# Attention and channel mix on one core: the first batch worked in halves of its heads

## The chip, the cores and the metric

The kernel runs on one core of a Trainium2 chip. The metric is the device time of one execution in microseconds; the median of the runs is compared. The engines are PE (TensorE), ACT (ScalarE), DVE (VectorE), POOL (GpSimd) and SP (SyncE, which only issues DMAs here). PE writes into PSUM, which the kernel divides into two rings of tiles: three `s` tiles of 2 x 512 columns and two `mm` tiles of 512.

## The reference

Two layers follow each other. The first is attention with a mask by blocks of 64, over 8 batches of 8 heads, 576 tokens and 64 dimensions; the second mixes each token with the one before it and runs through two matrices with a squared relu and a sigmoid gate:

```python
scores = scale * np.matmul(q, k.transpose(0, 1, 3, 2))
scores = np.where(block_i >= block_j, scores, -1000000000.0)
attn = np.exp(scores - np.max(scores, axis=-1, keepdims=True))
attn = attn / (np.sum(attn, axis=-1, keepdims=True) + 1e-09)
x = np.matmul(attn, v)                      # heads side by side: 512 channels
...
xk = mu_k * x + (1.0 - mu_k) * x_prev
xr = mu_r * x + (1.0 - mu_r) * x_prev
k = np.maximum(xk @ w_k, 0.0)
v = k * k @ w_v
r = 1.0 / (1.0 + np.exp(-(xr @ w_r)))
out = r * v
```

## The kernel before, in words

The work is cut into some 950 named tasks, each on one engine. For each batch there are, in order of dependence:

- loads of q and k (SP, two of each, 576 KB, each with four heads) and of v; they go to a ring of six `ld` tiles, and a load waits until the cast that read its tile before is done;
- casts to 16 bit (L255 and L251, on POOL, DVE or ACT, into `nl` and `vo` tiles);
- "turns" (L367): nine PE transposes of a q or k tile into an `s` tile, and a copy out of it into `qkt` (one of 1152 columns, for batch 0 two of 576);
- scores (L431): 12 tasks of four or eight 64x64 matmuls, each into an `s` tile, and the exponential of each on ACT (L441), which frees the tile;
- sums (`av S`, L483): 60 matmuls with a matrix `pick` of ones, that leave the row sums of the exponentials in part of one `s` tile; then products with v (`av A`, `av B`, L492), 40 matmuls each, in two further `s` tiles;
- on DVE: the sums turned (L520), reciprocals (L525), copies between partitions (L255/L251), per product a transpose that spreads them (L551) and the norm that multiplies (L561 and L565) into `xt`;
- the token differences (L587, DVE or POOL) and the mixes into XK and XR (L603, DVE): one instruction for each of four groups of 128 channels.

For batch 0 the 12 score tasks are two times six: the first six need only the first half of each copied turn. All 12 stand ahead of the one set of sums.

The second layer works on chunks of 512 tokens. A chunk has eight key products (`pk`, L650: four matmuls with WK into an `mm` tile, then relu and square), four gate products (`pr`, L672, then a tanh on ACT) and four value products (`pv`, L700: eight matmuls with WV, then the output on DVE, L708, and a store). The first key product needs the mixes of all four channel groups of batch 0 and two of the four casts of w_k.

What sets the order is a table, `ORDER`: task numbers in the order in which they are issued. Each engine takes its own tasks in that order and waits at each for what it needs; so a waiting instruction holds all that stands behind it on its engine. `PLACE` is a string that names the engine of each task that may go to several. A number with "+n" in `ORDER` puts n dummy matmuls on an identity (L264) ahead of that task on PE. Tasks of the kinds in `SHARED` (differences, mixes, squares, casts, copies of reciprocals) are tied: one on POOL waits for the last such one on DVE that was issued ahead of it.

Of the kernel before, what the change touches and what calls it, by code (L numbers as in the profile page):

```python
# [24 lines left out]
3 4 5+9 13 14 7 15+1 18 19 0 6 20+5 22 8 9 21 17 104 10+2 12 63+2 1 11  # L25
64 61 62 67+1 68 105 16 47+1 48 57+1 58 106 107 69 70 59 60 49+1 50 55
56 53 54 29 100 101 96 97 98+1 99 25 30 26 51 52 65+1 66 102 92 93 94 2
95 71 74 75 77 23 24 103 112 113 73 80 122 123 76 114+2 115 81 165 166
72+4 78 79 157 158 87 90 126 127 120+7 121 167 116 168 134 117 27 28
124+2 31 82 88 125 83 85 118+1 119 91 32 33 34 557 558 135 554 555 132  # L30
133 86 161 162 128 129 130 84 569 570 159 160 563 169 170 564 571 566
163 171 572 37 131 136 567 559 35 164 36 172 108 109 179 568 180 197 198
573 89 551 552 139 38 560 140 141 143 191 142 574 192 561 137 144 45 46
577 578 556 110 581 199 200 582 111 41 42 553 138 145 146 565 562 181
182 575 576 579 580 177 195 196 43 44 185 186 178 39 40 238 589 152 147
150 148 590 155 189 187 188 583 584 149 183 193 242 190 243 586 587 153
239 151 184 295 230 194 244 245 592 593 231 173 234 174 201 204 240 156
598 599 205 154 613 614 241 307 206 235 232 233 610 611 612 616 600 299
236 617 618 619 207 620 615 607 608 595 609 175 591 588 237 208 202 596
597 308 258 209 176 259 601 602 621 622 604 605 603 260 261 296 303 304  # L40
606 300 203 210 211 221 369 226 212 266 585 623 624 267 625 626 309 248
633 634 310 227 256 252 253 213 217 219 223 630 631 257 262 263 250 264
265 663 664 251 228 297 298 636 246 594 272 273 222 637 249 268 254 225
255 627 363 628 657 658 220 360 629 313 214 224 364 301 215 632 269 270
438 635 361 362 271 305 306 642 659 643 644 274 276 302 331 639 332 640
660 661 329 330 645 646 654 655 277 278 279 216 218 317 638 280 283 284
665 666 318 247 662 314 656 648 649 366 290 651 652 653 365 650 281 229
641 647 333 334 275 282 667 677 668 678 674 675 311 370 337 439 338 335
336 315 316 371 669 670 285 286 432 289 367 368 287 671 672 291 327 328
319 293 321 322 707 708 288 680 681 320 292 325 294 326 323 683 684 685  # L50
312 695 696 686 687 688 324 689 690 698 699 700 339 342 390 391 382 383
704 705 691 692 693 694 706 343 344 679 345 433 340 380 381 346 347 701
711 712 341 429 430 702 703 440 435 676 394 395 709 350 710 697 490 713
714 348 349 355 384 378 379 388 724 725 389 726 715 392 385 398 393 372
716 717 436 437 358 396 399 721 397 353 376 356 351 386 377 718 722 387
739 740 719 400 742 743 354 736 737 733 727 734 359 357 735 728 352 755
738 744 756 403 404 405 407 373 741 431 434 467 374 673 465 466 468 751
752 729 745 746 406 493 449 450 747 375 401 408 411 445 446 682 730 494
748 443 749 750 496 402 451 731 732 452 409 410 753 762 754 455 456 763
764 457 458 463 464 420 422 426 499 795 796 428 421 491 444 412 765 425  # L60
766 414 453 454 757 758 416 413 759 459 460 419 424 447 448 461 760 761
441 462 768 780 781 427 769 500 469 472 497 782 423 473 417 474 418 792
793 777 778 774 775 789 790 791 779 475 495 720 797 798 415 471 478 479
# [718 lines left out]
```

## Time and profile before

| | |
|---|---|
| median of 3 runs | 258.75 us (258.35 to 261.7) |
| the profiled execution | 258.47 us, of which 256.7 us are the profile's span |
| PE busy | 245.5 us (96%), 2710 matmuls, 41 of them dummies |
| DVE busy | 191.9 us (75%) |
| ACT busy | 178.8 us (70%) |
| POOL busy | 95.0 us (37%) |
| DMA | 46.96 MB, mean 183 GB/s |

PE's busy share is high in every slice, also in the first ones, where dummies and waits for data lie between its matmuls; it is 78 to 91% in the four stretches of 10 us up to 40 us, and over 95% after them but for the last. The granted TensorE clock is full throughout. To read the time, one asks from when PE's work is unbroken, what stands ahead of that moment, and where PE waits later.

### The profile page before, as it was taken

Reading aid. Unit: us, or ns where it says so; the run is one execution under the profiler, and the core shown is the slowest. Engines: PE = TensorE matmul, PEld = TensorE weight load, DVE = VectorE, ACT = ScalarE, POOL = GpSimd, SP = SyncE. Lnnn points to the kernel's source line nnn. Section 1 sums busy time; section 2 is a strip of 40 time slices with the busy share of each in tenths; the row PEclk is TensorE's granted clock in tenths of the full one; section 3 lists DMA queues with packets and bytes.
Section 4 is the critical chain, followed back from the end, with each engine's and each line's share of the span. In section 5 each row is a group of like instructions: output and inputs, shape, how many; then the busy total and the mean of one; then the engine's idle time right before and its main releaser. Section 6 shows DMA issues by size and latency. Waiting matters only on the chain.

```text
span 256.7 us, 6535 instructions
## 1 busy us (share of the span) xinstructions
PE 245.5 (96%) x2710; PEld 121.7 (47%) x2710; DVE 191.9 (75%) x275; ACT 178.8 (70%) x247; POOL 95.0 (37%) x81
## 2 busy tenths in 40 slices
PE   7887989999999999999999999999999989999995
PEld 3445535544655455444554545454444544444443
DVE  2535999999899989979696899757985786654313
ACT  1597786999868868859788678796789820550630
POOL 1122636773076015540533048306411362420730
PEclk9999999999999999999999999999999999999999
DMA  7999977999899919997951999759917004003104
GB/s 246 363 253 251 368 275 186 280 343 263 266 300 207 223 44 252 228 221 152 252 108 41 234 203 242 169 127 237 183 68 190 4 0 166 0 1 123 43 23 182
DMA packets 93150, 46.96 MB, mean 183 GB/s; under 512 B 80696, under 2 KB 80960, under 8 KB 93120
## 3 DMA queue, kind: packets, MB, share of 16 engines
q1 hardware_dynamic: 93120, 46.54, 74.6%
q8 instruction: 21, 0.34, 0.6%
q14 instruction: 9, 0.07, 0.1%
HBM read 33.56 MB, written 9.44 MB: 168 GB/s over the span
## 4 chain that ended last, share of the span: by engine, by line
PE 79%; DVE 10%; DMA 6%; issue 2%; ACT 1%; SPq 0%; DVEq 0%
PE t_mm L650 24%; PE t_mm L700 23%; PE t_mm L672 12%; PE t_s L431 7%; PE t_s L492 7%; DMA t_ld<-in_q_dram 4%; PE t_s L483 4%; PE t_s L367 3%; DMA t_ld<-in_k_dram 3%; DVE t_rt L551 2%; DVE XK L603 2%; DVE t_qkt L255 1%; DVE t_xt L565 1%; DVE t_d L587 1%; DVE WV L256 1%
## 5 line engine op out<-in xcount | busy, mean ns | idle before, releaser
L441 ACT ACTIVATE t_e<-t_s 128x1024 f16<-128x1024 f32 (+1 forms) x96 | 88.3, 983 | 19.2 <-PE t_s L431 17.1
L650 PE MATMUL t_mm<-XK,WK 128*128 128x512 f16 x288 | 68.5, 379 | 0.4 <-DVE XK L603 0.3
L638 POOL TENSOR_TENSOR t_k<-t_kr 128x512 f16<-128x512 f32 x39 | 42.1, 1097 | 69.5 <-ACT t_kr L628 51.4
L700 PE MATMUL t_mm<-WV,t_k 128*128 128x512 f16 (+1 forms) x296 | 66.5, 374 | 0.1
L628 ACT ACTIVATE t_kr<-t_mm 128x512 f32<-128x512 f32 x57 | 33.8, 598 | 24.8 <-PE t_mm L650 24.0
L700 PEld LDWEIGHTS <-t_k 128*128 128x128 f16 x296 | 27.9, 98 | 32.6 <-issue 1.9
L708 DVE SCALAR_TENSOR_TENSOR t_o<-t_t,t_mm 128x512 f32<-128x512 f32 (+1 forms) x37 | 24.8, 670 | 24.6 <-PE t_mm L700 16.4
L650 PEld LDWEIGHTS <-WK 128*128 128x128 f16 x288 | 26.6, 97 | 33.4 <-issue 6.0
L672 PE MATMUL t_mm<-WR,XR 128*128 128x512 f16 x144 | 35.4, 380 | 0.0
L255 POOL CAST t_nl<-t_ld 128x1152 bf16<-128x1152 f32 x15 | 18.6, 1257 | 41.9 <-DVE XR L603 25.3
L431 PE MATMUL t_s<-t_qkt 64*64 64x512 bf16 (+7 forms) x640 | 31.5, 290 | 2.8 <-ACT t_e L441 2.0
L681 ACT ACTIVATE t_t<-t_mm 128x512 f32<-128x512 f32 x36 | 21.4, 602 | 13.7 <-PE t_mm L672 13.5
L603 DVE SCALAR_TENSOR_TENSOR XK<-t_d,MU,t_xt 128x576 f16<-128x576 f32 (+2 forms) x40 | 29.0, 760 | 0.1
L603 DVE SCALAR_TENSOR_TENSOR XR<-t_d,MU,t_xt 128x576 f16<-128x576 f32 (+2 forms) x40 | 28.0, 722 | 0.1
L431 PEld LDWEIGHTS <-t_qkt 64*64 64x64 bf16 x640 | 14.9, 106 | 20.7 <-issue 16.9
L492 PE MATMUL t_s<-t_e,t_vo 64*64 64x64 f16 (+7 forms) x640 | 22.8, 285 | 1.1 <-DVE t_xt L561 1.0
L551 DVE STREAM_TRANSPOSE t_rt<-t_rc 128x1152 f32<-128x1152 f32 x16 | 22.0, 1374 | 2.0 <-ACT t_rc L251 1.5
L587 POOL TENSOR_TENSOR t_d<-t_xt 128x1152 f32<-128x1152 f32 x8 | 18.4, 2301 | 9.3 <-DVE t_xt L565 4.8
L492 PEld LDWEIGHTS <-t_vo 64*64 64x64 f16 x640 | 15.9, 107 | 10.4 <-issue 4.1
L672 PEld LDWEIGHTS <-XR 128*128 128x128 f16 x144 | 12.9, 98 | 16.3 <-issue 3.0
L255 DVE COPY t_qkt<-t_s 128x1152 bf16<-128x1152 bf16 (+1 forms) x13 | 14.9, 1166 | 6.5 <-PE t_s L367 6.2
L565 DVE TENSOR_TENSOR t_xt<-t_s,t_rt 128x1024 f32<-128x1024 f32 x16 | 19.4, 1213 | 0.1
(41 smaller groups left out, 189.0 us busy)
## 6 DMA issues: line engine op xcount, KB each, us to landing
t_ld<-in_v_dram SPq DMA_DIRECT2D x32, 288.0 KB, 4.3
out_dram<-t_o SPq DMA_DIRECT2D x35, 256.0 KB, 2.3
t_ld<-in_q_dram SPq DMA_DIRECT2D x10, 576.0 KB, 5.9
t_ld<-in_k_dram SPq DMA_DIRECT2D x10, 576.0 KB, 6.5
t_ld<-in_k_dram SPq DMA_DIRECT2D x12, 288.0 KB, 5.4
t_ld<-in_q_dram SPq DMA_DIRECT2D x12, 288.0 KB, 4.2
t_ld<-in_moe_w_k_dram SPq DMA_DIRECT2D x4, 512.0 KB, 8.3
t_ld<-in_moe_w_v_dram SPq DMA_DIRECT2D x4, 512.0 KB, 6.9
```

The costliest lines, as they stand in the source:

```text
L255: return e.tensor_copy(dst, src)
L431: nc.tensor.matmul(PS[g * D:g * D + D, x, col:col + n], qkt[rows, ka:ka + D], qkt[rows, qa:qa + n], start=True, stop=True)
L441: nc.scalar.activation(new(ebuf[key])[:, :, 0:width], new(m)[:, :, 0:width], AF.Exp, scale=ISQ)
L492: nc.tensor.matmul(dst(slice(y * D, (y + 1) * D), u, x, q0, n), new(vo_buf[b])[u * D:u * D + D, 2 * x + y, t], new(ebuf[key])[u * D:u * D ...
L551: nc.vector.transpose(new(rt[x])[:, 0:2 * W].rearrange("p (n r) -> p n r", r=QC), new(rc)[:, x].rearrange("p u n -> p (u n)").unsqueeze(2) ...
L603: return nc.vector.scalar_tensor_tensor((XK, XR)[kr][:, cc, g:g + w], new(d)[:, u * n + at - lo:u * n + at - lo + w], MU1[:, kr, cc:cc + 1 ...
L628: nc.scalar.activation(new(kr), new(m), AF.Relu)
L638: return e.tensor_tensor(dst(), KR, KR, ALU.mult)
L650: nc.tensor.matmul(ps, WK[:, cc, jc * P:(jc + 1) * P], XK[:, cc, at:at + CH], start=(cc == 0), stop=(cc == CCn - 1))
L672: nc.tensor.matmul(ps, XR[:, cc, g % R:g % R + P], WR[:, cc], start=(cc == 0), stop=(cc == CCn - 1))
L700: nc.tensor.matmul(ps[:, 0:w], k2[:, jc, jt * P:(jt + 1) * P], WV[:, jc, cols], start=(jc == 0), stop=(jc == JCn - 1))
L708: nc.vector.scalar_tensor_tensor(new(o)[:, 0:w], new(tb)[:, cols], 1.0, new(m)[:, 0:w], ALU.add, ALU.mult)
```

## The change

The first batch is worked by halves of its heads, as they are loaded: half 0 is heads 0 to 3, half 1 heads 4 to 7.

- Its six first score tasks now take the heads of one q and one k load (`a, e = (y, g ^ x) if b == 0`) and need both copies of their turns; the six others take the other loads.
- A new function `add_first` takes the place of `add_av` for it. For each half it makes the sums (60 matmuls a half, with a new matrix `only` that has ones in one half of the partitions: 120 instead of 60 in all), in one half each of one shared `s` tile; the products (40 matmuls a half, as many as before) in the two `mm` tiles, which are those of the key products, and in what is left of the shared `s` tile; and then reciprocals, copies, one transpose and a norm in three instructions.
- The loads of its v are cut by head, in eight DMAs instead of four.
- The differences and mixes of batch 0 go by its halves: channel groups 0 and 1 after the first norm, 2 and 3 after the second.
- `ORDER` and `PLACE` are new throughout. The dummies are 31 instead of 41. Of the squares 30 (before 16) are on DVE, 24 (39) on POOL and 18 (17) on ACT; of the casts of q and k 5 (8) are on DVE, 24 (15) on POOL and 3 (9) on ACT; of the relus 11 (15) are on DVE.

The diff without the two tables:

```diff
+    only = consts.tile([P, 2, 2 * QC], F16)
+    nc.vector.memset(only, 0.0)
+    for u in range(2):
+        nc.vector.memset(only[u * D:u * D + D, u, QC:QC + 1], 1.0)
...
         def jobs(d):
+            if b == 0:
+                return [(d[u * D:u * D + D, x * S:x * S + S].rearrange(
+                    "p (t d) -> p t d", d=D),
+                    v[b, 4 * i + 2 * x + (u ^ x)].rearrange(
+                        "(t p) d -> p t d", p=D))
+                    for x in range(2) for u in range(2)]
...
-                        ka = where(1, g, y, t * D)
-                        qa = where(0, g, y, q0)
+                        a, e = (y, g ^ x) if b == 0 else (g, y)
+                        ka = where(1, a, e, t * D)
+                        qa = where(0, a, e, q0)
...
-        deps = [evac[b, g, n, part if b == 0 else 0]
-                for g in range(2) for n in range(2)]
+        deps = [evac[b, g, n, y]
+                for g in ((part,) if b == 0 else range(2))
+                for n in range(2) for y in range(2 if b == 0 else 1)]
...
+    def add_first(half, mS):
+        every = [u for u in pieces_of(0, 0) if u[1][0] == half]
...
+        late = [p for p in every if p[1][1:4:2] != (0, 0)]
+        tail = [p for p in every if p[1][1:4:2] == (0, 0)]
+        mA = [plan.buf("mm") for _ in range(2)]
+        def fnS(eng, me):
+            PA = new(mS)[:, half]
...
+                        for u in range(2):
+                            runs.append((
+                                2 * (u ^ x) + x, a - j * cw, z - j * cw, j,
+                                new(ebuf[key])[:, x,
+                                               col + a - q0:col + z - q0],
+                                (t, q0), only[:, u, QC - j:2 * QC - j]))
...
+        sums = add(f"av 0 0 {'PS'[half]}", "PE", fnS,
+                   [ready[key] for key in keys], [mS] + ebs)
...
+        def fnA(eng, me):
+            unread(me, new(mA[0]))
+            products(tail, lambda r, x, q0, n: new(mS)[
+                r, x, QW + half * D:QW + (half + 1) * D])
+            products(late, lambda r, x, q0, n: new(mA[x])[
+                r, q0 - D:q0 - D + n])
+        av = add(f"av 0 0 {'AB'[half]}", "PE", fnA,
+                 [sums, cast["v", 0, half]],
+                 mA + [mS] + ebs + [vo_buf[0]])
...
+        t2_ = add(f"t2 0 {half} 0", "DVE", t2, fixed, [rc, rt])
+        def norm(eng, me):
...
+            nc.vector.tensor_tensor(
+                dst[:, :, 1:1 + D],
+                new(mS)[:, :, QW + half * D:QW + (half + 1) * D],
+                by[:, :, 0:D], ALU.mult)
+            for x in range(2):
+                nc.vector.tensor_tensor(
+                    dst[:, x, 1 + D:1 + S], new(mA[x])[:, 0:S - D],
+                    by[:, x, D:S], ALU.mult)
+        evac["x", 0, 0, half] = add(
+            f"norm 0 {half} A", "DVE", norm, [sums, av, t2_],
+            [mS, rt, xt_buf[0]] + mA)
...
-                cc = 2 * u + f
+                cc = 2 * u + f if b else 2 * f + u
...
-        add_av(b)
+        if b:
+            add_av(b)
+        else:
+            sums = plan.buf("s")
+            for half in range(2):
+                add_first(half, sums)
```

Three places show how the tables move the work. In the rows, `t_ld`, `t_nl`, `t_vo`, `t_s`, `t_mm` are the rings' tiles, `t_d` the differences, `t_e` the exponentials; the line numbers of the changed kernel are other ones.

SP, from the sixth load of a tile on (now from the seventh). Before:

```order
L272 DMA t_ld_63<-in_moe_w_k_dram 128x2x512
L272 DMA t_ld_58<-in_q_dram 128x2x576
L272 DMA t_ld_59<-in_k_dram 128x2x576
L272 DMA t_ld_60<-in_v_dram 64x18x64 x2
L272 DMA t_ld_61<-in_q_dram 128x2x576
L272 DMA t_ld_62<-in_v_dram 64x18x64 x2
L272 DMA t_ld_58<-in_q_dram 128x2x576
```

Now:

```order
L277 DMA t_ld_58<-in_q_dram 128x2x576
L277 DMA t_ld_59<-in_q_dram 128x2x576
L277 DMA t_ld_60<-in_v_dram 64x9x64 x4
L277 DMA t_ld_61<-in_v_dram 64x9x64 x4
L277 DMA t_ld_62<-in_k_dram 128x2x576
L277 DMA t_ld_63<-in_q_dram 128x2x576
L277 DMA t_ld_58<-in_k_dram 128x2x576
L277 DMA t_ld_59<-in_moe_w_k_dram 128x2x512
```

The first load of w_k moved from ahead of v to behind v and three loads of batch 2; eight loads of q and k and the two of v are ahead of it.

DVE, between the sums of batch 0 and the first key products. Before:

```order
L551 STREAM_TRANSPOSE t_rt_117<-t_rc_112 128x1152
L561 TENSOR_TENSOR t_xt_103<-t_s_154,t_rt_117 128x2x64
L565 TENSOR_TENSOR t_xt_103<-t_s_152,t_rt_117 128x2x512
L603 SCALAR_TENSOR_TENSOR XK<-t_d_121,MU_176,t_xt_103 128x576
L587 TENSOR_TENSOR t_d_122<-t_xt_103 128x1152
L603 SCALAR_TENSOR_TENSOR XK<-t_d_121,MU_176,t_xt_103 128x576
L603 SCALAR_TENSOR_TENSOR XK<-t_d_122,MU_176,t_xt_103 128x576 x2
```

Now:

```order
L656 STREAM_TRANSPOSE t_tt_108<-t_s_152 128x288
L664 RECIPROCAL t_rc_113<-t_tt_108 128x36
L733 SCALAR_TENSOR_TENSOR XR<-t_d_121,MU_176,t_xt_103 128x576
L733 SCALAR_TENSOR_TENSOR XK<-t_d_121,MU_176,t_xt_103 128x576
L260 COPY t_rc_113<-t_rc_113 32x18 x4
L684 STREAM_TRANSPOSE t_rt_117<-t_rc_113 128x1152
L692 TENSOR_TENSOR t_xt_103<-t_s_152,t_rt_117 128x2x64
L697 TENSOR_TENSOR t_xt_103<-t_mm_158,t_rt_117 128x512
L697 TENSOR_TENSOR t_xt_103<-t_mm_159,t_rt_117 128x512
L260 CAST t_nl_69<-t_ld_58 128x2x9x64
L717 TENSOR_TENSOR t_d_122<-t_xt_103 128x1152
L733 SCALAR_TENSOR_TENSOR XK<-t_d_121,MU_176,t_xt_103 128x576
```

The second half's sums, norm and difference stand behind the first half's mixes, with a cast of batch 2 between; both differences of batch 0 are on DVE, where one was on POOL. Two mixes of the second half follow this piece, then the first key product can run.

ACT, ahead of the first relu of a key product (`t_kr`). Before:

```order
L441 ACTIVATE t_e_91<-t_s_152 128x1024
L251 COPY t_qkt_74<-t_s_153 128x1152
L251 CAST WR<-t_ld_63 128x1024
L251 CAST t_vo_80<-t_ld_60 128x1152
L441 ACTIVATE t_e_92<-t_s_153 128x1024
L441 ACTIVATE t_e_93<-t_s_154 128x1024
L628 ACTIVATE t_kr_126<-t_mm_159 128x512
```

Now:

```order
L457 ACTIVATE t_e_91<-t_s_152 128x2x320
L256 COPY t_qkt_74<-t_s_154 128x1152
L256 CAST WK<-t_ld_62 128x2x512
L256 COPY t_qkt_74<-t_s_153 128x1152
L758 ACTIVATE t_kr_126<-t_mm_158 128x512
L256 COPY t_rc_112<-t_rc_112 32x36 x2
L457 ACTIVATE t_e_92<-t_s_154 128x1024
L758 ACTIVATE t_kr_128<-t_mm_158 128x512
```

All 24 exponentials of batches 0 and 1 and one of the casts of w_k, which were on POOL and DVE, now stand on ACT ahead of the first relu.

74 lines of the change are left out of this document (68 added, 6 removed), and 105 rows, old and new, of the table ORDER.

## The prediction

> **What bounds the kernel now.** I read the windows first, then the chain that ended last, then the groups of instructions by shape, and the timeline where two engines meet. In the windows each row has the stretch, its length and the busy time of PE, PEld, DVE, ACT and POOL, then the granted TensorE clock.
>
> ```profile
> 10.00:20.00 10.00, 8.36 (x103) 4.25 (x100) 4.71 (x6) 9.02 (x12) 3.33 (x3) 1.00 1.13 284
> 20.00:30.00 10.00, 7.92 (x163) 4.92 (x160) 7.52 (x11) 7.29 (x10) 3.38 (x3) 1.00 1.11 289
> 30.00:40.00 10.00, 9.09 (x120) 4.62 (x123) 9.79 (x12) 7.76 (x9) 4.59 (x3) 1.00 0.77 280
> 38.00:58.00 20.00, 19.85 (x294) 10.55 (x293) 19.61 (x28) 17.45 (x24) 13.75 (x13) 1.00 0.96 275
> ```
>
> From 38 us on PE is full: 19.85 of 20 us, and it loses another 1.04 us only near 206 (its row is in term D). So the time is made of two things: how late PE becomes full, with how much of its work done by then, and what it loses after. Before 38 us the chain of waits says what it is late for.
>
> ```profile
> 35.33 1.36 issue
> 36.69 1.55 DVE XK L603 x2
> 38.28 1.46 PE t_mm L650 x6
> 39.74 0.78 PE t_s L431 x24
> ...
> 41.49 0.50 PE t_s L367 x9
> 41.99 0.86 PE t_mm L650 x4
> ...
> 43.89 1.15 PE t_s L367 x18
> ...
> 45.91 1.36 PE t_s L483 x60
> ```
>
> A DVE chain (batch 0's norms, differences and mixes; L603 its last link) ends in the first key products. Of the eight matmuls of the first two, six run from 38.28 to 39.74; the other two came before (0.43 us at 0.86 for four). So the first key product stands at 38.28 - 0.43 = 37.85 in a PE stream that is unbroken from there.
>
> **Term A, PE work that now stands ahead of the first key product.** In the order of before, three of batch 1's scores, three of batch 2's turns and batch 1's sums follow that product; in the new order they precede it. The chain prices them: 0.78 (x24), 0.50 and 1.15 (three turns), 1.36 (x60), together **-3.8 us** after PE is full. The new first batch needs 120 instead of 60 matmuls for its sums, since each is made for one half of the partitions: 1.36 us more on PE. They fall ahead of the first key product, where PE waits for ACT and DVE anyway (8.36 and 7.92 of 10 us, dummy matmuls of L264 included), so I cost them at nothing; without that cover they cost 1.36.
>
> **Term B, when the first key product can start.** It still needs XK of both halves and two weight casts, so I follow DVE and ACT. Loads first:
>
> ```profile
> 4.24 0.76 DVE L255 CAST t_nl<-t_ld 128x1152 bf16<-128x1152 f32 x1 [2.35 <-DMA t_ld<-in_q_dram]
> 6.00 0.76 DVE L255 CAST t_nl<-t_ld 128x1152 bf16<-128x1152 f32 x1 [1.01 <-DMA t_ld<-in_q_dram]
> 17.46 1.04 SPq L272 DMA_DIRECT2D t_ld<-in_v_dram  x1
> t_ld<-in_v_dram SPq DMA_DIRECT2D x1, 288.0 KB, 7.6
> ```
>
> Before, the last piece of batch 0's v is issued at 17.46 and lands 7.6 us later, at 25.06, behind eight q and k loads, one weight load and the other v. In the new order the same eight and two stand there without the weight load. A load of 576 KB takes 6.00 - 4.24 = 1.76 us, so one of 512 KB 1.56: v is complete at 25.06 - 1.56 = 23.5. (SP issues eight pieces of v instead of four; it is ahead of the transfers, so that costs nothing. The weight load moved behind lands five loads later with another, near 33.7, ahead of its cast at 38.5.) DVE casts it (1.0) ahead of the first half's norm, so from 24.5 DVE is one serial chain, costed by these groups (count, busy us, mean ns of one):
>
> ```profile
> L565 DVE TENSOR_TENSOR t_xt<-t_s,t_rt 128x1024 f32<-128x1024 f32 x16 | 19.4, 1213 | 0.1
> L561 DVE TENSOR_TENSOR t_xt<-t_s,t_rt 128x128 f32<-128x128 f32 x16 | 4.6, 288 | 1.1
> L587 DVE TENSOR_TENSOR t_d<-t_xt 128x1152 f32<-128x1152 f32 x8 | 10.8, 1351 | 0.1
> L551 DVE STREAM_TRANSPOSE t_rt<-t_rc 128x1152 f32<-128x1152 f32 x16 | 22.0, 1374 | 2.0 <-ACT t_rc L251 1.5
> L525 DVE RECIPROCAL t_rc<-t_tt 128x72 f32<-128x72 f32 x8 | 4.8, 601 | 0.2
> L255 DVE COPY t_rc<-t_rc 32x36 f32<-32x36 f32 x20 | 4.8, 242 | 0.4
> L520 DVE STREAM_TRANSPOSE t_tt<-t_s 128x288 f32<-128x288 f32 x8 | 3.8, 478 | 2.6 <-PE t_s L431 1.1 <-ACT t_nl L251 0.8 <-PE t_s L483 0.7
> 33.19 0.81 DVE L603 SCALAR_TENSOR_TENSOR XK<-t_d,MU,t_xt 128x576 f16<-128x576 f32 x1
> 33.91 1.35 DVE L587 TENSOR_TENSOR t_d<-t_xt 128x1152 f32<-128x1152 f32 x1
> L255 DVE CAST t_vo<-t_ld 128x1152 f16<-128x1152 f32 x2 | 2.0, 1006 | 0.0
> ```
>
> Norm 1.6 (its large part now in two), difference 1.35, mix 0.81, sums turned 0.48, reciprocals 0.60, two mixes 1.62, four copies 0.97, transpose 1.37, norm 1.6, a cast of batch 2 at 0.76, difference 1.35, three mixes 2.43: 14.9 us, to **39.4**. The sums that it needs at 28 us are on PE in time. ACT independently:
>
> ```profile
> 9.34 0.63 ACT L251 COPY t_qkt<-t_s 128x576 bf16<-128x576 bf16 x1
> 12.80 10.48 ACT L441 ACTIVATE t_e<-t_s 128x1024 f16<-128x1024 f32 x12 [0.24 <-PE t_s L431]
> L251 ACT COPY t_qkt<-t_s 128x1152 bf16<-128x1152 bf16 x7 | 8.0, 1147 | 1.4 <-PE t_s L367 1.4
> L251 ACT CAST WR<-t_ld 128x1024 f16<-128x1024 f32 x1 | 1.0, 1048 | 0.0
> ```
>
> It starts its exponentials at about 9.1 (the second load is there at 6.00; cast, turn, copy and first score take three more us) instead of 12.80. Until the weight cast that the first key product needs it has 24 exponentials (10.48 / 12 = 0.87 each: 21.0), three half copies (1.9), five whole ones (5.7) and the cast (1.05): 29.6, to 38.7, and with about 0.8 of waiting for scores whose PSUM tiles the exponentials themselves free, **39.5**. Both chains agree: 39.5 against 37.85 is **+1.65 us**. Bounds: +0.7 if ACT never waits and DVE's instructions overlap at their ends; +3.7 if DVE loses 2 us to POOL. How it could:
>
> ```profile
> 34.05 2.10 POOL L255 CAST WK<-t_ld 128x1024 f16<-128x1024 f32 x1 [1.60 <-DMA t_ld<-in_k_dram]
> 35.18 3.05 DVE L603 SCALAR_TENSOR_TENSOR XK<-t_d,MU,t_xt 128x576 f16<-128x576 f32 x3
> ```
>
> A cast of 1.04 us on POOL took 2.10 beside a DVE difference, and the mix behind it was held until POOL was done: three mixes took 3.05 instead of some 2.25. That is the "issue 1.36" of the chain, most of it this wait. The Trainium skill (SBUF — State Buffer, "SBUF: two separate sides") states it as an exclusive lock between VectorE and GpSimd, held for the whole instruction, on VectorE operations with two SBUF inputs. This row agrees; by that rule each of the four POOL casts that the new order places beside DVE's chain would cost up to its whole 1.1 us, which is the second rival's mechanism.
>
> **Term C, what PE loses after that.** The new order gives DVE more of the squares and ACT the relus, and its three s buffers are all held by batch 1's sums and products until its norms. Three waits, by the groups above and these:
>
> ```profile
> L630 DVE TENSOR_SCALAR t_kr<-t_mm 128x512 f32<-128x512 f32 x15 | 10.1, 681 | 8.4 <-PE t_mm L650 8.2
> L638 DVE TENSOR_TENSOR t_k<-t_kr 128x512 f16<-128x512 f32 x16 | 13.6, 853 | 7.7 <-ACT t_kr L628 7.7
> L256 DVE TENSOR_SCALAR WV<-t_ld 128x1024 f16<-128x1024 f32 x2 | 1.3, 684 | 0.0
> ```
>
> First: an ACT copy that waits for DVE's reciprocals stands ahead of the exponential that frees a buffer. DVE: mix, weight cast, turn, reciprocals, 2.6 us to 42.1; copies and exponential on ACT to 43.5. PE by then has done three key products and two scores, 3.1 us, to 42.6: 0.9 lost. Second: a score waits for the second norm of batch 1: ten DVE steps, 10.2 us, to 52.3; PE has five key products (4.3), two sets of 40 products (1.3 each, near the sums' 1.36) and three scores (0.8) from 43.5, to 51.2: 1.1 lost. Third: the first value product needs the last square and WV cast on DVE, 6.8 us later at 59.1; PE has seven scores (1.8), four pr products (3.4) and a turn (0.5), to 58.0: 1.1 lost. That is 3.1; about half of these 21 steps overlap the one before by some 0.07 (the mix at 33.19 ends at 34.00, the difference behind it starts at 33.91), which takes back 0.8, and 38 to 58 loses 0.15 already: **+2.1 us**. Bounds +0.5 (small differences of long sums) and +4.5 (each wait a collision longer). Behind each waiting PE instruction the whole PE queue stands.
>
> **Term D, the wait near the end.**
>
> ```profile
> 206.01 0.28 DVE L561 TENSOR_TENSOR t_xt<-t_s,t_rt 128x128 f32<-128x128 f32 x1
> 206.35 1.42 PE L492 MATMUL t_s<-t_e,t_vo 64*64 64x64 f16 x40 [1.04 <-DVE t_xt L561]
> ```
>
> The last batch's second products wait 1.04 us for the first norm. In the new order one pr and seven key products stand between, 8 x 0.86 = 6.9 us, more than turn, reciprocals, copies, transpose and first norm instruction need (3.2): **-1.0 us**. It is 0 if another wait in the new table takes its place.
>
> Sum: -3.8 + 1.65 + 2.1 - 1.0 = -1.05. The profiled execution took 258.47 us, 256.7 of span and 1.8 around it; its own time less 1.05 is **257.4 us**. It lies 0.3 below the median of the runs shown, 258.75, well inside their spread to 261.7. A measurement of this kernel can tell about 2% (5 us) from no change, so this counts as none.
>
> **Rivals.** (1) Everything that is brought forward is swallowed: the first key product needs mixes of both halves, so working by halves starts it no earlier, and B and C reach 3.8 with D at 0: 258.5 us. For it speaks that DVE is already at 9.79 of 10 us in 30 to 40; against it, that ACT really starts 3.7 us earlier. (2) Slower: DVE's chain from 24.5 to 59 us becomes the bound because POOL's casts and differences hold it. Each meeting costs about 1.04; one uses up the 1.05 gained, from the second on it is slower, and three give 257.4 + 3.1 = 260.5 us. For it: the 1.36 us above, and eight DVE operations there with two SBUF inputs. Against it: in 38 to 58 DVE is busy 19.61 us now, with PE hardly losing anything. (3) The waits of C mostly close and B is at its lower bound: -3.8 + 0.7 + 0.5 - 1.0 = -3.6, 254.9 us. For it: ACT is ahead of its old place by the 3.7 us throughout; against it, that both chains of B end at the same 39.5, so that both would have to be shorter.
>
> **How the numbers follow.** Chances: forecast 0.40 (its own range 256.2 to 258.4), everything swallowed 0.18, collisions 0.25, waits close 0.17. The sum of the lower bounds is -3.8 + 0.7 + 0.5 - 1.0, the same 254.9; of the upper ones -3.8 + 3.7 + 4.5 + 0 = +4.4, 262.9. Leaving out a tenth at each end, and since the new table moves all later work too, I take 254.0 to 261.2. Faster by over 2% is under 253.3: a third of rival 3 and a little of the forecast, 0.08. Slower by over 2% is over 263.6: six collisions or a new wait late, 0.08. Within 2%: 0.84.
>
> **What would show it.** Right: the first key product (XK, WK) on PE at about 39.5 us with the sums of batch 1 before it; exponentials from about 9.1 us; v's second cast on DVE at 23.5; PE idle of half a us to one in front of a score near 43 and near 52, and before the first value product near 59, released by ACT and DVE; no 1 us wait for a norm near 205. Wrong: a first key product before 38.5 or after 41.5; PE idle of over 4 us in all in 40 to 60; DVE mixes of 1.5 us and more beside POOL casts in 24 to 40 (rival 2); or PE waits of over 1 us after 70 us, which the sum holds to be the same as now.

## The result, and the profile after

The changed kernel takes 271.44 us (median of 4 runs, 270.82 to 272.43) against 258.55 for the kernel before, run beside it: ratio 1.047, 95% interval 1.038 to 1.056. It is slower by 12.9 us; 257.4 was forecast, and 261.2 was the upper end. The profiled execution took 270.82 us, 269.0 of span, against 258.47 and 256.7. Runs of one kernel differ by the TensorE clock that they were granted on average (0.979 to 0.994 in the four of the changed kernel), so the clock is named wherever a number hangs on it.

I read the windows first, by stage. Kernel before:

```profile
0.00:30.00 30.00, 24.09 (x300) 13.00 (x300) 14.98 (x28) 19.28 (x24) 7.41 (x12) 1.00 1.02 289
30.00:60.00 30.00, 29.07 (x413) 15.22 (x413) 29.36 (x37) 25.95 (x33) 19.96 (x15) 1.00 0.94 287
60.00:100.00 40.00, 39.87 (x512) 21.42 (x513) 37.46 (x51) 33.21 (x45) 12.90 (x12) 1.00 0.93 211
100.00:160.00 60.00, 60.00 (x727) 28.59 (x720) 51.34 (x76) 46.55 (x67) 23.63 (x20) 1.00 0.97 190
160.00:220.00 60.00, 58.96 (x611) 27.96 (x609) 45.14 (x70) 40.02 (x58) 19.86 (x15) 1.00 0.55 124
```

The same windows of the changed kernel (busy time of PE, PEld, DVE, ACT and POOL, then clock, DMA share and GB/s):

```profile
0.00:30.00 30.00, 23.04 (x382) 13.55 (x383) 13.81 (x33) 20.36 (x23) 10.19 (x14) 1.00 1.00 314
30.00:60.00 30.00, 24.79 (x364) 13.07 (x368) 27.88 (x42) 24.62 (x33) 7.51 (x6) 0.94 0.80 211
60.00:100.00 40.00, 36.41 (x400) 19.15 (x389) 35.70 (x46) 28.47 (x38) 19.89 (x14) 1.00 1.00 226
100.00:160.00 60.00, 54.84 (x756) 27.57 (x753) 51.41 (x69) 44.66 (x62) 26.36 (x20) 1.00 1.08 196
160.00:220.00 60.00, 59.70 (x624) 28.38 (x623) 50.01 (x73) 40.64 (x63) 17.03 (x12) 1.00 0.52 116
```

The difference shows in PE's busy time, row by row: PE idles 1.05 us more up to 30, 4.28 more in 30 to 60, 3.46 more in 60 to 100, 5.16 more in 100 to 160, and 0.74 less after that; 13.2 in all for 12.3 us of span. So there are two losses, a head (5.3) and a stretch from 60 to 160 us (8.6) for which the prediction had nothing.

**The head.** The timeline of DVE in the changed kernel (start, length, engine, line, operation, and in brackets the idle time before it with what ended that), where the prediction let the first half's norm follow the cast of v:

```profile
23.61 0.72 DVE L260 CAST t_vo<-t_ld 128x1152 f16<-128x1152 f32 x1
29.70 0.29 DVE L692 TENSOR_TENSOR t_xt<-t_s,t_rt 128x128 f32<-128x128 f32 x1 [5.38 <-PE t_s L627]
29.91 1.28 DVE L697 TENSOR_TENSOR t_xt<-t_mm,t_rt 128x512 f32<-128x512 f32 x2
```

The cast is on time (23.5 was forecast), the norm is not: it waits 5.38 us for L627. Those are sums, and the first half's had run from 18.20 to 19.63. PE shows which they are:

```profile
28.22 1.43 PE L627 MATMUL t_s<-t_e,only 128*32 128x288 f16 x60
...
35.12 0.41 PE L446 MATMUL t_s<-t_qkt 64*64 64x512 bf16 x4
38.92 0.58 PE L269 MATMUL t_mm<-identb 128*128 128x512 bf16 x1 [3.39 <-DVE t_xt L697]
...
43.38 1.43 PE L499 MATMUL t_s<-t_e,pick 128*32 128x288 f16 x60
...
45.34 1.90 PE L780 MATMUL t_mm<-XK,WK 128*128 128x512 f16 x8 [0.20 <-ACT WK L256]
```

The sums of 28.22 are the second half's. They go to the second bank of the s tile in which the first half's sums have the first bank, and the early blocks of both halves' products lie behind the sums in both banks; the first instruction of a norm (L692) reads both. The waiting norm starts as the last of these 60 matmuls ends (28.22 + 1.43 = 29.65). At 38.92 a dummy matmul waits 3.39 us in front of a score whose own tile ACT had emptied by 35.5: the program counts an mm tile as free for dummies once its last reader is listed, and that reader, the second half's norm, had still to run. The first key product stands at 45.34, where 39.5 was forecast. Batch 1's sums (43.38) do precede it, as term A says. In the kernel before it stood at 37.55 (the prediction had worked out 37.85 from the chain):

```profile
37.55 2.19 PE L650 MATMUL t_mm<-XK,WK 128*128 128x512 f16 x8 [0.26 <-DVE XK L603]
```

ACT starts its exponentials at 10.00 (9.1 was forecast), and then stands still where PE does:

```profile
10.00 4.37 ACT L457 ACTIVATE t_e<-t_s 128x640 f16<-128x640 f32 x5 [0.44 <-PE t_s L446]
...
40.18 1.02 ACT L457 ACTIVATE t_e<-t_s 128x1024 f16<-128x1024 f32 x1 [3.52 <-PE t_s L446]
...
44.22 1.07 ACT L256 CAST WK<-t_ld 128x1024 f16<-128x1024 f32 x1
```

**Behind 60 us.** The two largest of PE's waits there, and DVE ahead of the first of them:

```profile
132.65 1.42 PE L508 MATMUL t_s<-t_e,t_vo 64*64 64x64 f16 x40 [2.55 <-DVE t_tt L536]
...
156.71 1.42 PE L508 MATMUL t_s<-t_e,t_vo 64*64 64x64 f16 x40 [2.48 <-DVE t_tt L536]
```

```profile
126.51 1.54 DVE L733 SCALAR_TENSOR_TENSOR XR<-t_d,MU,t_xt 128x576 f16<-128x576 f32 x2
130.79 0.69 DVE L838 SCALAR_TENSOR_TENSOR t_o<-t_t,t_mm 128x512 f32<-128x512 f32 x1 [2.74 <-DMA out_dram<-t_o]
131.40 0.81 DVE L733 SCALAR_TENSOR_TENSOR XR<-t_d,MU,t_xt 128x576 f16<-128x576 f32 x1
132.13 0.47 DVE L536 STREAM_TRANSPOSE t_tt<-t_s 128x288 f32<-128x288 f32 x1
```

Batch 4's and batch 5's first products write their early blocks beside their own sums, so they wait until DVE has turned these (L536). At 130.79 DVE itself waits 2.74 us for a store that was issued only at 126.00, since the other three output tiles are held by stores that the table lists later. At 156.71 the product stands straight behind its sums, and DVE reaches the turn after mixes, an output and a cast. The rest of the 8.6 us are waits of 0.4 to 0.9 us between 60 and 98.

### The profile page after: what moved, and what is told of

The parts are those of the page before. It is cut to its first block, busy times and chain, and to the rows that moved or that the text cites. A ratio compares the mean times of both kernels' runs of the same rounds, so it can differ in the third digit from the quotient of the medians.

```text
span 269.0 us, 6611 instructions
## 1 busy us (share of the span) xinstructions
PE 244.5 (91%) x2760; PEld 122.9 (46%) x2760; DVE 205.8 (76%) x296; ACT 176.4 (66%) x246; POOL 88.0 (33%) x72
## 4 chain that ended last, share of the span: by engine, by line
PE 69%; DVE 15%; ACT 6%; DMA 4%; issue 3%; POOL 1%; SPq 0%; DVEq 0%; POOLq 0%
PE t_mm L780 21%; PE t_mm L830 19%; PE t_mm L802 10%; PE t_s L446 7%; PE t_s L508 6%; ACT t_e L457 4%; DVE XK L733 3%; DVE XR L733 3%; PE t_s L499 2%; PE t_s L372 2%; ACT t_qkt L256 2%; DMA t_ld<-in_k_dram 2%; DMA out_dram<-t_o 2%; DVE t_qkt L260 2%; DVE t_d L717 1%
## 5 line engine op out<-in xcount | busy, mean ns | idle before, releaser
L457 ACT ACTIVATE t_e<-t_s 128x1024 f16<-128x1024 f32 (+1 forms) x96 | 89.8, 976 | 26.1 <-PE t_s L446 20.4
L758 ACT ACTIVATE t_kr<-t_mm 128x512 f32<-128x512 f32 x61 | 35.9, 598 | 29.3 <-PE t_mm L780 27.2
L768 POOL TENSOR_TENSOR t_k<-t_kr 128x512 f16<-128x512 f32 x24 | 27.5, 1155 | 70.1 <-ACT t_kr L758 47.0
L260 POOL CAST t_nl<-t_ld 128x1152 bf16<-128x1152 f32 x24 | 29.9, 1251 | 41.3 <-DMA t_ld<-in_q_dram 13.9
L733 DVE SCALAR_TENSOR_TENSOR XK<-t_d,MU,t_xt 128x576 f16<-128x576 f32 (+2 forms) x40 | 33.5, 870 | 1.1 <-POOL t_d L717 1.0
L768 DVE TENSOR_TENSOR t_k<-t_kr 128x512 f16<-128x512 f32 x30 | 23.3, 787 | 8.5 <-ACT t_kr L758 8.2
L508 PE MATMUL t_s<-t_e,t_vo 64*64 64x64 f16 (+7 forms) x560 | 19.9, 284 | 5.0 <-DVE t_tt L536 5.0
L567 DVE STREAM_TRANSPOSE t_rt<-t_rc 128x1152 f32<-128x1152 f32 x14 | 19.3, 1376 | 2.1 <-ACT t_rc L256 1.8
L256 ACT COPY t_qkt<-t_s 128x1152 bf16<-128x1152 bf16 (+1 forms) x13 | 13.2, 1021 | 10.2 <-DVE t_qkt L260 7.1
L508 PEld LDWEIGHTS <-t_vo 64*64 64x64 f16 x560 | 14.2, 107 | 12.1 <-issue 7.0
```

The costliest lines, as they stand in the source:

```text
L260: return e.tensor_copy(dst, src)
L457: nc.scalar.activation(new(ebuf[key])[:, :, 0:width], new(m)[:, :, 0:width], AF.Exp, scale=ISQ)
L508: nc.tensor.matmul(dst(slice(y * D, (y + 1) * D), u, x, q0, n), new(vo_buf[b])[u * D:u * D + D, 2 * x + y, t], new(ebuf[key])[u * D:u * D ...
L733: return nc.vector.scalar_tensor_tensor((XK, XR)[kr][:, cc, g:g + w], new(d)[:, u * n + at - lo:u * n + at - lo + w], MU1[:, kr, cc:cc + 1 ...
L758: nc.scalar.activation(new(kr), new(m), AF.Relu)
L768: return e.tensor_tensor(dst(), KR, KR, ALU.mult)
```

## The experiments

Theory W: the norm's wait for the other half's sums makes the head late. Rival M: the dummies that wait do. For the later loss, theory K: it is a knock-on of the late head. Theory T: it belongs to the later part of the new table itself. Medians, and the ratio to the kernel before with its 95% interval where the runs allow one:

| run | median us | ratio |
|---|---|---|
| e1_norm_first | 269.76 | |
| e2_no_late_dummies | 270.26 | |
| e3_both | 267.40 | 1.030 (1.021 to 1.038) |
| b1_late_head | 262.68 | 1.012 (1.002 to 1.022) |
| h1_new_head_old_rest | 263.53 | 1.021 (1.016 to 1.025) |
| h2_old_head_new_rest | 271.39 | 1.050 (1.045 to 1.056) |
| h3_norm_first_old_rest | 260.85 | 1.009 (1.006 to 1.013) |
| h4_both_old_rest | 258.66 | 0.999 (0.996 to 1.002) |
| h5_head_with_dummies | 260.60 | 1.008 (1.004 to 1.011) |
| h6_dummies_that_run | 259.09 | 1.000 (0.997 to 1.004) |
| s1_store_early | 269.93 | 1.042 (1.038 to 1.047) |
| x1_store_unheld | 269.45 | 1.039 (1.031 to 1.048) |
| x2_product_later | 268.32 | 1.034 (1.027 to 1.042) |
| x3_head_store_product | 263.08 | 1.012 (1.003 to 1.021) |
| p1_old_engines | 291.79 | 1.126 (1.118 to 1.134) |
| p2_engines_and_store | 294.85 | 1.129 (1.122 to 1.136) |
| f1_mended_pr_between | 257.47 | 0.997 (0.995 to 1.000) |
| f2_before_pr_between | 258.01 | 0.999 (0.996 to 1.003) |

### Who waits for whom in the sums tile

e1_norm_first: in the changed kernel's table the second half's sums (79) and the score behind them go behind the first half's copies, transpose, cast of v and norm (78). Each engine's own list of instructions is the same, word for word.

```diff
-117+1 118 29 30 79 133 134 76 77 162 26 78 163
+117+1 118 29 30 76 77 162 26 78 79 133 134 163
```

> The changed kernel; in the order the first half's copies, transpose, v cast and norm are only listed ahead of the second half's sums instead of behind them. Every engine issues the same instructions in the same order as before this edit; what turns round is who waits for whom in the shared sums tile: now the second sums wait for the first norm. Theory W (the norm's 5.38 us wait for the other half's sums makes the head late): the norm starts near 24.6 us instead of 29.70, the second norm near 34 instead of 37.98, and the first key product near 41.4 instead of 45.3. Rival M (the dummy matmuls that wait in an mm tile make it late): DVE is earlier, but PE still waits about 3 us for a dummy, the key product moves by less than 1.5 us. For the time: theory K (the 8 us lost after 60 us are a knock-on of the late head) expects most of both back, about 260 us; theory T (they belong to the new table itself) expects only the head's 4 us, about 267.

DVE in this run, and then PE:

```profile
24.10 0.28 DVE L692 TENSOR_TENSOR t_xt<-t_s,t_rt 128x128 f32<-128x128 f32 x1
...
31.54 0.48 DVE L656 STREAM_TRANSPOSE t_tt<-t_s 128x288 f32<-128x288 f32 x1 [3.20 <-PE t_s L639]
```

```profile
36.92 0.38 PE L269 MATMUL t_mm<-identb 128*128 128x512 bf16 x1 [1.92 <-DVE t_xt L697]
...
42.40 1.90 PE L780 MATMUL t_mm<-XK,WK 128*128 128x512 f16 x8 [0.20 <-ACT WK L256]
```

The norm starts at 24.10 and the first key product at 42.40, 2.94 us earlier, although no engine got another list. So W holds for the head. The second norm came at 35.98, not at 34: DVE now waits 3.20 us at 31.54 to turn the second half's sums, for products (L639) of that half, which are listed ahead of the turn and write the same bank. It is the same tile once more; listing that turn first was not tried. The profiled run took 264.53 us at clock 1.00, the three others 269.47 to 270.40 at 0.98, so the median says little of the head. In this trace PE idles 5.2 us between 60 and 160 us, where it idled 8.8 in the changed kernel: a part of the later loss seems to go with the head, the larger part stays.

e2_no_late_dummies: the ten dummies behind the first half's products go.

```diff
-121+1 ... 117+1 ... 119+1 ... 131+2 ... 123+1 ... 172+1 ... 176+1 ... 562+1 ... 202+1
+121 ... 117 ... 119 ... 131 ... 123 ... 172 ... 176 ... 562 ... 202
```

> The changed kernel without the ten dummy matmuls that its table puts behind the first half's products. Theory W: the first norm still starts near 29.70 and DVE's mixes end where they did, so the key product gains at most the 1 us by which ACT's weight cast is later than DVE's last mix; 270 us. Rival M: the 3.39 us PE wait at 38.92 goes and with it ACT's 3.52 us idle time; the key product comes near 42, the TensorE clock keeps 1.00 or nearly, and the time falls by 3 us and more, to 268 or less.

The first key product came at 43.76, 1.6 us earlier, between the 1 us that W allowed and the 3 us of M. The norm still started at 29.18, and PE still waits 2.11 us for the second norm at 38.30, now with a score that takes the shared sums tile. The four runs lie between 266.90 and 271.47 us, too far apart to tell the time's change from none. So M is real and the smaller part; the clock fell all the same (0.89 and 0.77 in 30 to 40 and 40 to 50).

e3_both: both edits.

> Both edits together, the first norm listed ahead of the second sums and no dummy matmul behind the first half's products. Theory W with M as a smaller part: first key product near 40.5, half a us to 1 us earlier than with the norm's edit alone. Time: theory K about 259, theory T about 266.

```profile
38.97 1.43 PE L498 MATMUL t_s<-t_e,pick 128*32 128x288 f16 x60
40.40 0.60 PE L779 MATMUL t_mm<-XK,WK 128*128 128x512 f16 x2
```

40.40, as expected. The time is 267.4: the head gives back 4.0 us of 12.9, about what T expects (266) and far from K (259), and PE still idles 7.3 us between 60 and 160.

### Does a late head cost more later?

b1_late_head: the kernel before, with 20 dummies ahead of its first key product.

```diff
-124+2 31 82 88 125 83 85 118+1 119 91 32 33 34 557 558
+124+2 31 82 88 125 83 85 118+1 119 91 32 33 34 557+20 558
```

> The kernel before, with 20 dummy matmuls (identity weights, 512 columns) ahead of its first key product and nothing else changed: PE becomes full of its own work 20 x 0.22 = 4.3 us later. Theory K (a head that is 4 us late costs 8 us more later on, whatever the table): 267 to 271 us, with PE waits of over 1 us after 70 us. Theory T (the later losses belong to the new table): 4.3 us and no more, 262 to 263.

```profile
36.35 4.49 PE L264 MATMUL t_mm<-identb 128*128 128x512 bf16 x20
40.68 1.67 PE L650 MATMUL t_mm<-XK,WK 128*128 128x512 f16 x7
```

The key product stands 3.1 us later than in the profile before, not 4.3, since the work ahead of the dummies stood 0.9 us earlier in this execution; the profiled spans differ by 2.6 us (259.3 and 256.7). The medians differ by 4.25 us (262.68 and 258.43), but two of the four runs stood at clock 0.993 (264.11 and 264.39), and the two at 1.00 took 261.04 and 261.25. Nothing is lost later on: PE loses 0.12 us in 60 to 100, as it did without the dummies, and nothing in 100 to 160. K, with 267 and more, is out for the table before.

h1_new_head_old_rest and h2_old_head_new_rest exchange the later part. Up to the first key product (`562`, or `557` in the numbers of before) the table stays, behind it stands the other one's order, with its engines.

```diff
 173 92 127 128 164 165 176+1 88 141 27 28 177 95 93 96
-562+1 563 31 33 34 144 145 146 556 557 115 186
+31 32 33 34 562 563 559 560 94 574 575 568 569
```

> The changed kernel, its table kept up to the first key product (137 of 955 entries); all that follows in the order, and on the engines, of the table before. The head is that of the changed kernel, with its first key product at 45.3. Theory T (what PE loses behind 60 us belongs to the new table's later part): PE idle behind 60 us falls from 9 us to about 1, and the time to 271.4 - 8 = 263 or a little less. Rival K2 (the late head costs it in this kernel, if not in the one before): 269 and more.

> The kernel before, with its own first batch and its table kept up to its first key product (116 of 950 entries); all that follows in the order and on the engines of the new table. Its first key product stays near 37.5. Theory T: PE loses 5 us to 8 us between 60 and 160 although the head is as early as before, 264 to 267 us. Rival K2: 257 to 260.

PE in 60 to 160, h1 first:

```profile
60.00:100.00 40.00, 39.73 (x441) 20.14 (x440) 38.06 (x47) 34.51 (x47) 13.22 (x10) 1.00 0.93 230
100.00:160.00 60.00, 60.00 (x754) 29.17 (x756) 49.97 (x76) 46.00 (x65) 21.05 (x17) 1.00 0.94 186
```

```profile
60.00:100.00 40.00, 37.19 (x412) 19.29 (x412) 36.22 (x48) 30.64 (x41) 20.88 (x16) 1.00 1.03 238
100.00:160.00 60.00, 56.38 (x771) 28.75 (x770) 54.44 (x69) 45.11 (x63) 25.37 (x20) 1.00 1.03 190
```

With the old rest PE loses 0.3 us there although its first key product is as late as 46.2: 263.53 us, as T said. With the new rest it loses 6.4 us. The second run did not keep its head early, as I had expected: the new rest puts turns and sums of batches 1 and 2 ahead of the key product, and one of these turns waits 3.74 us for a POOL cast, so that the key product stands at 48.35. Its 271.39 is therefore no measure of the new rest alone; its idle time in 60 to 160 is. T stands, and in the changed kernel the rest costs 271.44 - 263.53 = 7.9 us, the head the other 4.9; the intervals of the two runs leave some 2.5 us either way, and PE's idle time (8.8 us in 60 to 160 in one, 0.3 in the other) says the same.

### The head by itself

h3_norm_first_old_rest and h4_both_old_rest are e1 and e3 with the old rest; h5 and h6 are h3 without one dummy (`172+1`) and without two (`123+1`, `172+1`).

> The changed kernel with the first half's norm listed ahead of the second half's sums, its table up to the first key product, and behind that the order and engines of the table before. First key product near 42.4, as with the norm's edit alone. Theory T: 5.5 us less than that edit alone in the same clock, so 259 us where the clock stays at 1.00 and 263 where it falls to 0.98. Rival K2: 264 and more, PE idle behind 60 us as before.

> As the one with the norm listed first and the old rest, and without the ten dummy matmuls behind the first half's products. First key product near 40.4. Theory T: 267.4 - 6 = 261 us. If this head were worth what was forecast for it, 257.4; so 261 says that the clock that it loses (0.985 to 0.994 with these dummies gone) eats the rest. Rival K2: 266 and more.

> The changed kernel with the norm listed ahead of the second sums and the old rest of the table, as in the run that gave 260.85, but of its dummy matmuls only the one ahead of a turn of batch 2, which waited 1.92 us in an mm tile, is taken out; the others stay. Without any of the ten late ones the TensorE clock was 0.83 in 30 to 40 us. If the clock is what that head loses (0.17 x 10 = 1.7 us): clock above 0.95 there, first key product at 40.5 to 41, 257.0 us. If the clock does not matter, 258.7 as without them. If another dummy takes over the wait, 260 and more.

> The mended head with the old rest (258.7 without late dummies, 260.8 with all, 260.6 with all but one that had not been the waiting one); here the two dummies in front of a score and a turn of batches 1 and 2, of which the first waited 1.92 us, are out, the other seven stay. If clock decides: no wait at 38, TensorE clock over 0.95 in 30 to 50, 257.0 us. If the dummies cost as much PE time as they keep: 258.7 to 259.5.

h3 gave 260.85, with the first key product at 43.75 instead of the expected 42.4 behind a clock of 0.86 in 30 to 40 us. h4 gave 258.66, 2.3 less than I had expected. In h5 I had taken out the wrong dummy, not the one that waits:

```profile
37.99 0.38 PE L268 MATMUL t_mm<-identb 128*128 128x512 bf16 x1 [1.92 <-DVE t_xt L696]
```

So h5 repeats h3 (260.60). h6 takes the right one out; six late dummies stay in it, not seven. Its profiled execution keeps the clock (first fence) where h4's loses it (second), and it is no faster, 259.09 against 258.66.

```profile
30.00:40.00 10.00, 7.86 (x168) 5.39 (x168) 8.12 (x15) 9.58 (x11) 1.15 (x1) 1.00 0.66 212
40.00:50.00 10.00, 8.72 (x76) 3.49 (x68) 9.22 (x17) 6.04 (x7) 5.06 (x5) 1.00 1.02 227
```

```profile
30.00:40.00 10.00, 7.47 (x139) 5.24 (x142) 8.83 (x16) 9.90 (x12) 0.92 (x1) 0.83 0.72 231
40.00:50.00 10.00, 9.52 (x100) 4.05 (x92) 9.22 (x16) 5.71 (x8) 5.74 (x6) 1.00 0.95 254
```

The two traces don't show that the dummies keep the clock. f1 below has h4's instructions in h4's order up to 200 us, without these dummies, and its profiled execution kept the clock too:

```profile
30.00:40.00 10.00, 6.80 (x164) 4.86 (x164) 8.91 (x16) 9.90 (x12) 1.15 (x1) 1.00 0.77 240
```

Over all runs the mean clock was 0.998 or more in ten of ten of h6, three of ten of h4 and eight of twelve of f1, which speaks for the dummies. The dip falls where PE waits for ACT and DVE in any case and costs next to nothing there: h4's three runs with the full clock took 258.45 to 258.74 us, the six at 0.993 258.47 to 259.09.

The head without its side effects (h4) is worth nothing, -0.1 us, interval -1.1 to +0.5. Its first key product:

```profile
40.50 2.06 PE L779 MATMUL t_mm<-XK,WK 128*128 128x512 f16 x8
```

Its parts agree: -3.8 of work ahead (term A), first key product at 40.50 instead of 37.55 (+2.95), 0.5 more idle behind it, nothing of term D with the old rest; -0.4.

### What in the later part costs

s1_store_early moves a store (`678`), x1_store_unheld another one (`637`), x2_product_later batch 5's first products (`406`) and a value product (`729`); x3_head_store_product is e3 with the edits of x1 and x2.

```diff
-687 387 388 346 ... 472 473 678 425 495
+687 678 387 388 346 ... 472 473 425 495
```

```diff
-673 370 640 367 440 ... 696 377 637 445 700
+673 370 640 637 367 440 ... 696 377 445 700
```

```diff
-406 457 409 410 466 467 498 726 412 413 356 727 448 729 730
+457 409 410 466 467 498 726 729 406 412 413 356 727 448 730
```

> The changed kernel with one entry of its table moved: the store of the third chunk's first output tile is listed 120 entries earlier, behind another store of that chunk; nothing else. Theory S (the 2.74 us that DVE waits at 128 to 130.8 for a store to land, since the three other output tiles are held by stores that the table lists later, is what makes PE wait 2.55 us at 132.65): DVE's wait goes, PE's falls below 0.5, the time falls by 2 us, to about 269.3. Rival: DVE is that late anyway, or the next wait takes it back; less than 0.7 us.

> The changed kernel with one store moved: that of the second chunk's second output tile (o0 in the trace's order), listed 68 entries earlier, ahead of the third chunk's outputs. The fourth output of that chunk, which waited 2.74 us for a store that had only just been issued, now gets a tile whose store is long done. Theory S: DVE does not wait there, PE's 2.55 us before batch 4's first products goes, 269 us. Rival (DVE is late by its other work): PE still waits 1.5 us and more there, 271.

> The changed kernel with one product moved: batch 5's first products stood straight behind their sums, and PE waits 2.48 us there until DVE has turned the sums, which share the bank; now three scores' worth and two value products (3.7 us of PE work that is ready) are listed between. Theory P: that wait goes, 269 us. Rival: DVE is the bound, the wait comes back at the products or at the next score; 271.

> Both edits on the head with the norm listed first and without late dummies (267.4 alone). Theories S and P: 267.4 - 5.0 = 262.4, PE idle behind 60 us below 3. If DVE's late work takes the time back: 265 to 267.

s1 was a slip: that store held nothing up, DVE waited 1.89 us at the same place as before, PE 1.71, and 269.93 is within the spread of the changed kernel. x1 frees the right tile; its DVE and PE at the place:

```profile
127.66 0.69 DVE L838 SCALAR_TENSOR_TENSOR t_o<-t_t,t_mm 128x512 f32<-128x512 f32 x1 [0.39 <-PE t_mm L830]
```

```profile
129.72 1.42 PE L508 MATMUL t_s<-t_e,t_vo 64*64 64x64 f16 x40 [0.40 <-DVE t_tt L536]
```

The store's 2.74 us are gone, and PE's 2.55 are 0.40. (Where nothing at this place was changed, PE's wait was 2.55, 1.71 in s1 and 1.57 in x2, so 1.2 to 2.2 us of it are the store's.) x2, at batch 5's products:

```profile
154.08 3.63 PE L830 MATMUL t_mm<-WV,t_k 128*128 128x512 f16 x16
157.63 1.42 PE L508 MATMUL t_s<-t_e,t_vo 64*64 64x64 f16 x40
...
160.39 1.36 PE L508 MATMUL t_s<-t_e,t_vo 64*64 64x512 f16 x33 [0.96 <-DVE t_xt L581]
```

The products no longer wait; 0.96 us of the 2.48 (1.70 in x1, which leaves this place alone) come back at the second ones. The medians fell by 2.0 (269.45) and 3.1 (268.32), with intervals that overlap the changed kernel's; the traces show the two waits gone. Together on the mended head (x3) they give 263.08 against 267.40, but not all of these 4.3 us are theirs, since the clock differs, 0.985 to 0.994 in the runs of e3 and 1.00 in all four of x3. In the profiles, e3 first:

```profile
100.00:160.00 60.00, 55.44 (x767) 28.05 (x765) 51.24 (x68) 43.82 (x62) 26.23 (x20) 0.97 1.06 190
```

```profile
100.00:160.00 60.00, 58.03 (x801) 29.07 (x794) 55.36 (x71) 46.97 (x67) 26.35 (x20) 1.00 1.09 202
```

PE idles 2.6 us less here and 0.7 more in 60 to 100, so about 2 us of the 5.0 expected are shown. Of the loss behind 60 us, 3.4 us in 60 to 100 and 2.0 in 100 to 160 remain, where less than 3 in all was expected, in waits of 0.7 to 1.6 us; these were not taken apart.

p1_old_engines changes only who does what (PLACE) behind the first key product, 55 squares and 19 casts, with the order untouched; p2_engines_and_store has s1's store besides.

```diff
-PADADPPDAAPDPAAPDDPDPPPPPDAADDPPPPPADDPPDPPPPAAAPDDDDDAAAAAAADADAA
+PPDADPADPAPDDADPDDPDPPAPPPAADDDDPPAADDPPAPPAPAAAPDDPDPAPAPAPAPAPAA
```

> The changed kernel with its order untouched; behind its first key product only the engines of squares and of the q, k and v casts are those of the table before where they differ (71 of them: 29 squares go to POOL and 14 leave it, 25 squares leave DVE and 11 come to it, 11 of 19 casts leave POOL). Theory E (the assignment makes DVE late in 80 to 160): PE idle behind 60 us falls from 9 to about 4, 266 us. Rival O (the order of the later part does it, or order and engines only work together): 270 and more.

> The two edits together: old engines for squares and casts behind the first key product, and the one store earlier. Theories E and S both right: 264. E wrong, S right: 269. Both wrong: 271.

PE's longest waits in p1 (what it waited for, us in all, times, longest; the second row is the head's dummies):

```profile
PE t_mm L830 <- POOL t_k L768: 5.7, 3, 4.0
PE t_mm L269 <- DVE t_xt L697: 3.8, 2, 3.2
PE t_s L372 <- POOL t_nl L260: 3.7, 3, 2.6
```

291.79 and 294.85: 20 and 23 us worse (it was 74 entries, not 71). Value products now wait for POOL's squares (5.7 us) and turns for POOL's casts (3.7). E fails, and rival O holds as far as it goes: in this order the old engines are worse than the new ones. It does not tell which of order and engines makes DVE late in the changed kernel.

### Term D alone

f1_mended_pr_between is h4, f2_before_pr_between the kernel before, each with two pr products of chunk 6 (`845`, `841` in the numbers of before) ahead of batch 7's second products (`532`).

```diff
-541 532 539 540 546 845 841 544
+541 845 841 532 539 540 546 544
```

> The mended head without late dummies and the old rest (258.7), and two of chunk 6's pr products (1.7 us of PE work) listed between batch 7's two product steps, where PE waited 1.04 us for the norm. If that wait ends nowhere else: 257.6 us. If the norms behind it, now 0.7 us later, are needed at once: 258.7.

> The kernel before with the same two entries moved and nothing else. The same 1.0 us: 257.6. Together with the other run it tells what the new first batch is worth without any of its side effects; by the two medians measured so far (258.7 and 258.7), nothing.

In f1 PE is full there, where h4 lost 1.04 us:

```profile
200.00:220.00 20.00, 20.00 (x202) 9.68 (x195) 16.96 (x25) 7.91 (x15) 8.08 (x6) 1.00 0.14 53
```

f1 takes 257.47 us, 0.997 of the kernel before (0.995 to 1.000), the lowest median here, by a hair. f2's profiled span is 255.3 against 256.7, but its median of 258.01 is that of the kernel before (257.98 beside it): a gain of 1 us is not shown by its runs. Between f1 and f2, which differ only by the first batch and the order up to the first key product, lie 0.5 us, less than their spread: the new first batch is worth nothing that these runs can tell.

## Why the prediction was wrong

**The later table at nothing.** The largest error, 7.9 of 12.9 us, is no term of the sum at all: term C ends at 59 us, and behind it only D was priced; PE waits of over 1 us after 70 us stood among the signs that would prove it wrong. That the new table moves all later work only widened the range. The new order itself (of the outputs, the stores, and the products straight behind their sums) was there to be followed. Two of its waits are shown with their causes (x1, x2); of the others only that they belong to the table (h1, b1).

**Term B.** The step that failed is "from 24.5 DVE is one serial chain", with "The sums that it needs at 28 us are on PE in time". I asked only whether the second half's sums would be ready to be turned, and not whether the first half's norm, whose tile they write, would have to wait for them. They ended at 29.65; the norm waited 5.38 us for them, and the first key product came 7.8 us later than before instead of 1.65. The Trainium skill (PSUM — Partial Sum Buffer, "PSUM bank collisions raise a hardware error") says that accesses of two engines must be kept apart by bank and group of 32 partitions, not by address; this case shows what keeping them apart costs, 5.38 us on a norm whose own columns nobody was writing (no run here tries it without the wait). With this and the dummies taken away (e3, h4) the key product stands at 40.4 to 40.5, and at 39.9 in f1: the chain of DVE and ACT itself was at most 1 us longer than forecast, within its bounds.

**Dummies.** I counted them among what PE does while it waits anyway. One of them waited itself, 3.39 us, with a score behind it that was ready; ACT then had 3.52 us without work.

**Term A** was right: the three scores, turns and sums do stand ahead, and h4's sum closes with -3.8. The second set of sums (1.43) was put at nothing because PE waits there in any case; in the changed kernel it is what the first norm waits for, and with the norm listed first its cost was not tested by itself.

**Term C** named three waits near 43, 52 and 59 us. The changed kernel was late as a whole and lost 0.21 us in 40 to 60; with the mended head (e3) there are 0.91 at 45 and 0.37 at 57, both of scores that wait for ACT. That is 1.3 of the 2.1 us: the kind was right, the size too large.

**Term D.** The wait at 206 went, and PE idles 0.74 us less from 160 to 220. Its worth by itself lies below what the runs tell.

**Rival 2** (mixes held by POOL) did not decide the head: the four mixes that start between 41.31 and 43.50 took about 0.8 us each. Ahead of the second late wait it shows:

```profile
148.12 3.20 DVE L733 SCALAR_TENSOR_TENSOR XK<-t_d,MU,t_xt 128x576 f16<-128x576 f32 x2
...
153.30 1.69 DVE L733 SCALAR_TENSOR_TENSOR XR<-t_d,MU,t_xt 128x576 f16<-128x576 f32 x1
```

Beside a square and two casts on POOL these three mixes took 4.9 us instead of 2.4. The 2.5 us more are as much as PE waits at 156.71. That this is what made DVE late there was not tested.

## What to carry to other kernels

Work by halves can lose in shared tiles what it gains by starting early: ask of every tile that a step reads who else writes it, by bank, and in which order the program lists the two, since that order decides who waits (e1). A filler instruction is free only while its own target is; ahead of work that is ready it delays everything behind it. When a change brings a whole new table, price the part behind the change too, or exchange the halves of old and new table, which here told some 5 us of head from some 8 us of rest in one run.

## What the runs showed of the hardware

The clock does not need one long gap to fall. In the changed kernel it is 0.94 and 0.89 around the 3.39 us wait, but h4 has 0.83 in 30 to 40 us with PE busy 7.47 of 10 and no wait over 0.69 us. The Trainium skill (TensorE: Matmul & The Clock Gate, "What's actually happening") puts the fall after an idle window of about 3.4 us; the first agrees, the second does not. Nor do the instructions alone decide: f1, with h4's own up to 200 us and waits of up to 0.71 us in 30 to 40, kept 1.00. What a lower clock costs depends on the kernel. h4 took 258.5 to 259.1 us at a mean clock of 0.993 and 258.5 to 258.7 with the full clock; beside it the kernel before took 260.3 to 260.9 at 0.993 and 257.5 to 259.8 with the full clock. Where the clock fell in those runs of the kernel before, no trace here shows.
